# Attention outputs of two position blocks in one run of 128 products, with other buffer counts, a shared tile and another order

## The chip, the cores and the metric

The kernel runs on one core of one Trainium2 chip. The metric is the device time of one execution in microseconds (us), taken as the median of several executions. The core has five engines: TensorE (PE, matrix products; its weight loads appear as PEld), VectorE (DVE), ScalarE (ACT), GpSimd (POOL) and SyncE (SP, here an issuer of DMAs). Products land in eight accumulation banks of 128 x 512 float32; DVE or ACT must read a bank before it can be filled again.

## What is computed

The block reads x (2048 tokens of 448 features), normalises it, and sends the result through two branches: sliding dilated attention with 16 heads of 28, in which a token sees itself and the seven tokens at distances 2, 4, ..., 14 before it, and a GELU feed-forward of width 1792. The second branch, through a SiLU, gates the first.

```python
def _A_ref(x, wqkv, wo):
    H = 16; Dh = D // H
    W, dil = 8, 2
    q, k, v = ...
    idx = pos[:, None] - (jnp.arange(W) * dil)[None, :]
    ...
    attn = _softmax(logits, axis=-1)
    o = jnp.einsum("bhsw,bhswd->bhsd", attn, vg)
    return o.transpose(0, 2, 1, 3).reshape(B, S, D) @ wo

def _B_ref(x, w1, b1, w2, b2):
    h = _gelu(x @ w1 + b1)
    return h @ w2 + b2

xn = _layernorm(x, axis=-1)
return x + _A_ref(xn, ...) * _silu(_B_ref(xn, ...))
```

## The kernel before

**Positions.** Even tokens come first, then the odd ones, so that the dilation of 2 becomes a window of eight neighbouring positions. There are 16 tiles of 128 positions and 4 chunks of 512 (chunk c holds tiles 4c to 4c+3). Attention walks over nine blocks (the table VIS), here called visits: each has four sub-blocks of 57 query positions (56 in visit 4), each of which needs 64 key positions. Visit 0 begins at position 0, visit 4 at 912, visit 5 at 1136, visit 8 at 1820.

**Products.** Most products run with the 128 x 128 array split into two row tiles of 64 rows, two banks side by side (`pair`): L581 q and k projections, L604 the v projection, L657 the first feed-forward product (its result goes through GELU on ACT at L661), L689 the second feed-forward product, L849 the output projection. The last two tiles use the whole array (L711, L857).

**A visit** has two parts:

- "S": `scores_of` makes 32 products of 57 columns (L756, row tiles of 64, 128 columns of weights) into four banks. The keys were spread before into a buffer `kd` (L641 on ACT or L643 on DVE). `weights_of` then takes the exponentials of each bank on ACT into a buffer E (L765), and DVE multiplies E by the window's mask (L771).
- "P": `values_of` makes 64 products P V (L785, array split into 64-row by 32-column tiles) from four E buffers and a values buffer v into two banks. `output_of` then works on each of the two banks on DVE: transpose (L794), reciprocal of the row sums (L798), transpose back (L803), and the multiplication that writes oT and frees the bank (L808).

The values go from the v projection through a scratch tensor in HBM (v_hbm) and are loaded back in the layout of a visit by two DMAs (L391, from SP or POOL). k and q are turned by transposing DMAs from SP into qkT.

**Order.** The kernel builds a list of tasks, each with an engine, a modelled cost, dependencies, buffers that it takes and gives, and a priority. `_Plan.run` schedules this list once, when the program is built: at each step it takes the task that can start first, or one that can start within 0.12 us of it and has a higher priority. The numbers in PRIO, LATER and NUDGE are those priorities (NUDGE by the task's number). The instructions are then emitted in the planned order, and every engine runs its own in that order, waiting on semaphores. Buffers come from pools; p_b is the eight banks. A pool marked fifo hands its buffers out in the order in which the tasks were listed. E has 8 buffers of 512 columns, v has 3. The pool p_f with one entry and a task on an engine called "CLK" keep 3.5 us between the end of one P task and the start of the next in the plan.

`VISITS` lists the parts of a group of visits: S0, S1, P0, S2, P1, S3, and so on. The feed-forward of chunks 0 and 1 (first product) comes first, then visits 0 to 5 as one group, the first product of chunk 2, visits 6 to 8, and that of chunk 3. Exponentials of a group wait for the GELUs before it and GELUs for the exponentials before them, since ACT has to load another table. In `attn`, each S part depends on the S part before it and on the P part of the visit two earlier; each P part depends on its four masked exponentials, its values and the P part before it.

xnT holds the normalised x, turned (features on partitions, positions along the columns); oT holds the attention output in the same layout. Both are tiles of 4 x 2048 columns of their own. xnT of chunk c is read by the projections of its tiles and by the first feed-forward product of that chunk; oT is read by L849 and L857.

Of the kernel before, what the change touches and what calls it, by code (L numbers as in the profile page):

```python
# [17 lines left out]
TILED = 30  # L18
BURST = 3.5
NUDGE = {  # L20
    84: 158, 140: -205, 166: -239, 224: 179, 265: -119, 391: -219, 425: 30, 447: -224, 491: 168, 498: 19,
    903: 27,
}
LAST = 352
SAME = 20
# [2 lines left out]
MASK_ON = ("DVE", 0.4)  # L28


def VISITS(bs):
    out = []
    for i, b in enumerate(bs):
        out.append(("S", b))
        if i:
            out.append(("P", bs[i - 1]))
    return out + [("P", bs[-1])]

class _Pool:
# [138 lines left out]
def kernel(  # L180
# [13 lines left out]
    P = 128  # L194
    S, D, H, DH, F = A_x.shape[1], 448, 16, 28, 1792
# [4 lines left out]
    KT = 4  # L200
# [6 lines left out]
    HALF = S // 2  # L207
# [24 lines left out]
    def sb(name, shape, dt=BF16):  # L232
        return const.tile(shape, dt, name=name)
# [9 lines left out]
    b1r = sb("b1r", [P, P])  # L243
    b1 = sb("b1", [P, NMT], F32)
    b2 = sb("b2", [P, D])
    xnT = sb("xnT", [P, KT, S])
    qkT = sb("qkT", [P, 2, G, PAD + S])
    v_tok = [sb(f"v_tok{t}", [P, 2, H // 2, 32]) for t in range(4)]
    v_hbm = dram.tile([BACK + S, H * 32], BF16, name="v_hbm")
    oT = sb("oT", [P, KT, S])  # L250
    ident = sb("ident", [P, P])
    eps_t = sb("eps_t", [P, 1], F32)
    half_t = sb("half_t", [P, 4], F32)
# [32 lines left out]


    PRIO = {
        "project": (111.5, -88, 18.5, -696,),
        "project2": (-23.5, 19.5, -594, -964,),  # L290
        "values": (-44, -423, -594, -735.5,),
        "attn": (359, 96.5, 62.5, 202.5, 5, 57.5, 182.5, 179.5, 223.5,),
        "ff1": (13.5, 120, 49, 24, 187, 87.5, 62.5, -96, 84.5, 398.5, 78, 73.5, 5.5, 35, 103.5,
            101.5, 228.5, 177.5, -12.5, 185, 115.5, 165, -11, 8.5, 65.5, 138, 132.5, 110.5,),
        "gelu": (136.5, 97, 104.5, 181,),
        "ff2": (147, -34.5, -129, 114.5, 103, 89, -829, 135, -9.5, 180.5, -80, 104, 9, 131, -305.5,
            -310.5,),
        "final": (-14, 2, 199.5, -16.5, -12, -2, 22.5, 203, -185.5, 65.5, -11.5, 162.5, 193.5, 134,
            130, 176,),
        "norm": (131, 11, 219.5, 294, 126, 78, 2.5, 146.5, 217, -20.5, 87, 237, 173.5, 157, 14.5,  # L300
            120.5,),
        "loads": (-74, -48, 129, 164.5, 47.5, 92.5, 83.5, 53.5,),
        "stats": (49, 32, 205.5, 205.5, -8, 159.5, 204.5, 62, 27, 91, -57, 69.5, 123.5, 176.5, 85,
            125,),
        "turn_x": (198, 4.5, 200, 12.5, 117, 30.5, -154, 79.5, 36.5, 99.5, 169.5, 65.5, 252.5, 141,
            91, 50.5,),
        "turn_qk": (9, 28.5, 28, 90.5, 18, 3, 179.5, -13.5, 189.5, 20.5, 214, 5.5, 109, 113.5, 54,
            138,),
        "move_v": (111.5, 21, 150.5, -65.5, -155.5, 32.5, 203, 59.5, 78.5,),
        "store_v": (122.5, 143.5, 17.5, 49.5, 111, 48.5, 78, -15, 175, 108.5, 186.5, 121, 197.5,  # L310
            108.5, 47.5, 176.5,),
        "spread": (169, 63, 206, 112.5, 78, 182.5, 161.5, 83.5, 132.5,),
        "copies": (187, 4, 219, 15.5, 90, 177, 88.5, 31, 29, 20.5, 182, 51, 204.5, 49.5, 24,),
    }
# [431 lines left out]
    def scores_of(b):  # L746
        q, n = VIS[b]
        own, ready = spread(b)

        def fn(banks):  # L750
            for s in range(4):
                for g in range(G):
                    for h in range(2):
                        r = slice(64 * h, 64 * h + 64)
                        c0 = (G * (s % 2) + g) * n
                        nc.tensor.matmul(banks[2 * h + s // 2][:, c0:c0 + n], buf(p_k, own)[r, g, s, :],  # L756
                                         qkT[r, 0, g, PAD + q + n * s:PAD + q + n * s + n], start=True, stop=True)
        return fn, [ready] + [t_qk[t] for t in range(q // P, (q + 4 * n - 1) // P + 1)], ((p_k, own, 0),)
# [16 lines left out]
    def values_of(b, exps):  # L775
        n = VIS[b][1]

        def fn(banks):
            for s in range(4):
                for g in range(G):  # L780
                    for h in range(2):
                        for a in range(2):
                            r = slice(NK * a, NK * a + NK)
                            c0, c1 = (4 * h + s) * n, (G * (s % 2) + g) * n
                            nc.tensor.matmul(banks[a][32 * g:32 * g + 32, c0:c0 + n], buf(*v_at[b])[r, s, 2 * g + h, :],  # L785
                                             buf(p_E, exps[2 * h + s // 2])[r, c1:c1 + n], start=True, stop=True)
        return fn, tuple((p_E, e, 0) for e in exps) + (v_at[b],)
# [25 lines left out]
            t_oT[t].append(o)  # L813

    last_visit = {"S": [], "P": []}
    state = {}
# [225 lines left out]
```

## Time and profile before

| what | value |
|---|---|
| three executions | 152.68, 152.21, 152.67 us (median 152.67) |
| profiled execution | 152.89 us, of which the span of instructions is 151.20 us |
| granted TensorE clock | 0.998 of full speed |
| L657, L689 products | 392 of each; 44.0 and 40.2 us busy |
| L581, L604, L849 products | 25.4, 13.7 and 12.9 us busy |
| one P V run (L785, 64 products), nine in all | 0.70 us from its first product's start to its last one's end |
| one run of scores (L756, 32 products), nine in all | 0.59 to 0.61 us in the same sense |
| exponential (L765), 128 x 456 | 558 ns, 36 in all |
| mask (L771), 128 x 456 | 390 ns, 36 in all |
| output of one P V bank on DVE (L794, L798, L803, L808) | 677, 251, 678 and 633 ns |
| y addition (L723), 128 x 448, which frees an L689 bank | 619 ns |

The page gives the busy time of each engine and the chain of work that ended last. Matmuls overlap in the array, so a group's busy time can be longer than the distance at which the groups follow each other; the timeline, which merges neighbouring instructions of a kind into one line with its start and its duration to the end of the last, shows that distance. Groups of instructions are named by line, engine and the tiles written and read; "[0.43 <-DVE oT L808]" behind a line is the idle time before it and what ended it.

### The profile page before, as it was taken

To read this page: it belongs to the slowest core of one execution; us is meant where nothing else is said; L and a number is where in the kernel's file an instruction comes from. 1 tells how busy PE (TensorE), PEld (TensorE's weight loads), DVE (VectorE), ACT (ScalarE), POOL (GpSimd) and SP (SyncE) were. 2 spreads that over 40 slices of the span, in tenths; PEclk is the share of its full clock that TensorE was granted. 3 is DMA by queue.
4 is the path that set the end of the run, shared out by engine and by line. 5 is a ranking of instruction groups with operands and counts; after the bars stand their busy time and mean duration, and the time that the engine had idled before them with its cause. 6 is when DMAs were issued, how large, how long until landed. Compare 5 with 4: busy or idle time off the path is not lost.

```text
span 151.2 us, 5214 instructions
## 1 busy us (share of the span) xinstructions
PE 145.9 (97%) x2169; PEld 75.9 (50%) x2169; DVE 114.2 (76%) x277; ACT 93.7 (62%) x167; POOL 20.1 (13%) x53
## 2 busy tenths in 40 slices
PE   7899999999999999999998999999999999999990
PEld 2544444544455555555545554445556445555460
DVE  3886850585738789999598998587998977995952
ACT  3455888429893595767744679788296497822020
POOL 7435440214440000021200000000000000000000
PEclk9999999999999999999999999999999999999999
DMA  4999968899998357169699983421120000001221
GB/s 138 335 295 345 164 137 144 261 239 297 186 166 153 74 74 139 49 125 228 134 200 192 195 190 101 112 72 41 34 65 4 2 0 4 4 0 61 62 96 31
DMA packets 37895, 19.47 MB, mean 129 GB/s; under 512 B 24888, under 2 KB 37119, under 8 KB 37871
## 3 DMA queue, kind: packets, MB, share of 16 engines
q1 hardware_dynamic: 37118, 17.58, 51.9%
q0 software_dynamic: 608, 1.44, 4.3%
q8 instruction: 17, 0.28, 0.8%
q10 hardware_dynamic: 144, 0.11, 0.3%
q14 instruction: 8, 0.06, 0.1%
HBM read 9.42 MB, written 3.94 MB: 88 GB/s over the span
## 4 chain that ended last, share of the span: by engine, by line
PE 85%; DMA 5%; DVE 4%; POOL 3%; issue 1%; ACT 0%; POOLq 0%
PE bank L657 28%; PE bank L689 25%; PE bank L581 10%; PE bank L849 6%; DMA qkT<-qk_tok 5%; PE bank L604 4%; PE bank L711 4%; PE bank L785 3%; PE bank L756 2%; POOL wo L340 1%; DVE dt L803 1%; PE bank L857 1%; DVE dt L794 1%; PE bank L499 1%; DVE kd L643 1%
## 5 line engine op out<-in xcount | busy, mean ns | idle before, releaser
L657 PE MATMUL bank<-xnT,w 64*128 64x512 bf16 x392 | 44.0, 376 | 0.0
L661 ACT ACTIVATE h<-bank,b 128x512 bf16<-128x512 f32 x56 | 34.1, 688 | 10.3 <-PE bank L657 10.0
L689 PE MATMUL bank<-w,h 64*128 64x448 bf16 x392 | 40.2, 349 | 0.0
L657 PEld LDWEIGHTS <-w 64*128 64x128 bf16 x392 | 18.8, 94 | 22.1
L689 PEld LDWEIGHTS <-h 64*128 64x128 bf16 x392 | 18.8, 94 | 16.3
L581 PE MATMUL bank<-w_in,xnT 64*128 64x448 bf16 (+1 forms) x212 | 25.4, 350 | 0.0
L765 ACT ACTIVATE E<-bank 128x456 bf16<-128x456 f32 (+1 forms) x36 | 16.8, 557 | 6.4 <-PE bank L756 6.4
L333 ACT CAST qk_tok<-bank 128x448 bf16<-128x448 f32 x27 | 13.2, 538 | 6.7 <-PE bank L581 6.6
L794 DVE STREAM_TRANSPOSE dt<-bank 128x480 f32<-128x480 f32 (+1 forms) x18 | 12.1, 673 | 4.5 <-PE bank L785 4.4
L581 PEld LDWEIGHTS <-xnT 64*128 64x128 bf16 (+1 forms) x212 | 10.5, 94 | 9.6 <-issue 0.7
L604 PE MATMUL bank<-w_in,xnT 64*128 64x448 bf16 (+1 forms) x106 | 13.7, 349 | 0.0
L849 PE MATMUL bank<-wo,oT 64*128 64x448 bf16 x112 | 12.9, 349 | 0.4 <-DVE oT L808 0.4
L803 DVE STREAM_TRANSPOSE dt<-rd 128x480 f32<-128x480 f32 (+1 forms) x18 | 12.1, 675 | 0.6
L445 DVE BATCH_NORM_STATS2 st<-x_sb 128x6 f32<-128x448 bf16 x16 | 9.6, 609 | 3.1 <-DMA x_sb<-in_A_x_dram 3.1
L808 DVE TENSOR_TENSOR oT<-bank,dt 128x456 bf16<-128x456 f32 (+1 forms) x18 | 11.4, 632 | 0.6
L771 DVE TENSOR_TENSOR E<-E,m_gen 128x456 bf16<-128x456 bf16 (+1 forms) x32 | 11.0, 390 | 0.0
L723 DVE TENSOR_TENSOR y<-bank,b 128x448 f32<-128x448 f32 x15 | 8.7, 619 | 2.4 <-PE bank L689 2.2
L333 ACT CAST v_tok<-bank 128x448 bf16<-128x448 f32 x12 | 6.0, 534 | 5.6 <-PE bank L604 3.6
L735 ACT ACTIVATE t<-y 128x448 f32<-128x448 f32 x12 | 6.7, 582 | 3.9 <-DVE y L723 3.9
L849 PEld LDWEIGHTS <-oT 64*128 64x128 bf16 x112 | 5.6, 94 | 5.6 <-issue 0.9
L480 DVE TENSOR_SCALAR xn<-x_sb,mv,rstd 128x448 bf16<-128x448 bf16 x16 | 6.4, 399 | 2.4 <-POOL rstd L468 2.3
L604 PEld LDWEIGHTS <-xnT 64*128 64x128 bf16 (+1 forms) x106 | 5.6, 94 | 4.7
(74 smaller groups left out, 134.7 us busy)
## 6 DMA issues: line engine op xcount, KB each, us to landing
v_hbm<-v_tok SPq DMA_DIRECT2D x14, 128.0 KB, 3.9
out_dram<-o SPq DMA_DIRECT2D x15, 112.0 KB, 2.4
v<-v_hbm SPq DMA_DIRECT2D x13, 128.0 KB, 3.5
w<-in_B_w_dram SPq DMA_DIRECT2D x2, 672.0 KB, 7.1
w_in<-in_A_wqkv_dram SPq DMA_DIRECT2D x3, 336.0 KB, 4.4
x_sb<-in_A_x_dram SPq DMA_DIRECT2D x4, 224.0 KB, 5.5
w<-in_B_w_dram SPq DMA_DIRECT2D x2, 448.0 KB, 6.4
w<-in_B_w_dram SPq DMA_DIRECT2D x2, 336.0 KB, 5.8
```

Of the source, the lines that this page charges most:

```text
L333: nc.scalar.copy(o, i)
L581: return nc.tensor.matmul(ps[:, :D], xnT[r, kt, cs], w, start=start, stop=stop)
L604: return nc.tensor.matmul(ps[:, :D], xnT[r, kt, k0:k0 + P], w, start=start, stop=stop)
L657: return nc.tensor.matmul(ps[:], w1[r, kt, ms], xnT[r, kt, cs], start=start, stop=stop)
L661: nc.scalar.activation(buf(p_h, own, i)[:], buf(p_b, own, i)[:], ACT.Gelu_apprx_tanh, bias=b1[:, mt:mt + 1])
L689: return nc.tensor.matmul(ps[:, :D], buf(*h_at[(c, mt)])[r, cs], w2[r, mt, :], start=start, stop=stop)
L765: nc.scalar.activation(buf(p_E, k)[:, :8 * n], buf(p_b, a, at + i)[:, :8 * n], ACT.Exp, scale=SCALE)
L771: nc.vector.tensor_tensor(out=E, in0=E, in1=m[:, :, :, :n].rearrange("p i g q -> p (i g) q"), op=ALU.mult)
L794: nc.vector.transpose(buf(p_dt, k)[:, :32 * m], buf(p_b, po, i)[:, :32 * m])
L803: nc.vector.transpose(buf(p_dt, d)[:, :32 * m].rearrange("p (b c) -> p b c", c=32), buf(p_rd, r)[:, :m].unsqueeze(2).to_broadcast((P, m, 32)))
L808: nc.vector.tensor_tensor(out=oT[:, a::2, q:q + 4 * n1], in0=buf(p_b, po, i)[:, :n].rearrange("p (l q) -> p l q", l=2), in1=buf(p_dt, d)[: ...
L849: return nc.tensor.matmul(ps[:, :D], oT[r, kt, t * P:(t + 1) * P], wo[r, kt, :], start=start, stop=stop)
```

## The change

- `VISITS` now groups visits by TOGETHER: (0, 1), (2, 3), (4, 5), (6, 7), (8). It lists the S parts of a group, then the P part of the group before: S0, S1, S2, S3, P01, S4, S5, P23, P45; S6, S7, S8, P67, P8.
- A P part of two visits is one task of 128 products into four banks, which waits for the masks and values of both visits; it gives back eight E buffers and two v buffers. The four outputs follow as before, each for a bank.
- An S part of visit b depends on the S part before it and on the P task of the latest visit up to b - 4 that has one listed already.
- E has 15 buffers of 456 columns, v has 4.
- xnT and oT become two views of one tile xT of 4 x 3072 columns: oT is columns 0 to 2047, xnT columns 1024 to 3071. So positions 1024 and up of oT lie on positions 0 to 1023 of xnT.
- The numbers in PRIO, LATER and NUDGE are others, which gives another order on every engine.

```diff
 NUDGE = {
-    84: 158, 140: -205, 166: -239, 224: 179, 265: -119, 391: -219, 425: 30, 447: -224, 491: 168, 498: 19,
-    903: 27,
+    51: -17, 100: 72, 158: 186, 160: 19, 169: -108, 170: 110, 184: -158, 227: -173, 230: -199, 398: -138,
+    428: -8, 461: 105, 892: 15,
 }
...
+TOGETHER = ((0, 1), (2, 3), (4, 5), (6, 7), (8,))
+
+
 def VISITS(bs):
-    out = []
-    for i, b in enumerate(bs):
-        out.append(("S", b))
-        if i:
-            out.append(("P", bs[i - 1]))
-    return out + [("P", bs[-1])]
-
+    out, left = [], []
+    for m in [m for m in TOGETHER if m[0] in bs]:
+        out += [("S", b) for b in m] + left
+        left = [("P", m)]
+    return out + left
...
-    xnT = sb("xnT", [P, KT, S])
+    xT = sb("xT", [P, KT, HALF + S])
+    xnT, oT = xT[:, :, HALF:], xT[:, :, :S]
...
-    oT = sb("oT", [P, KT, S])
...
-    p_E = ring("E", 8, [P, 512], fifo=True)
+    p_E = ring("E", 15, [P, 8 * NW], fifo=True)
...
-    p_v = ring("v", 3, [P, 4, H // 2, 32], fifo=True)
+    p_v = ring("v", 4, [P, 4, H // 2, 32], fifo=True)
...
-        "attn": (359, 96.5, 62.5, 202.5, 5, 57.5, 182.5, 179.5, 223.5,),
+        "attn": (95, 33.5, 174.5, 3, 187.5, 61, 136.5, 427, 178.5,),
...
-    LATER = {"swap": 159, "qk": -43.5, "v": 16, "gelu": 21.5, "exp": 188.5, "mask": -4724.5, "pv": 29.5, "recip": 183.5, "os": 346, "y": 166, "tanh": 151, "g": 147.5, "sg": -120.5, "o": 0}
+    LATER = {"swap": 231.5, "qk": 165, "v": 171.5, "gelu": 94, "exp": 96.5, "mask": -4417.5, "pv": 209.5, "recip": 201.5, "os": 234, "y": 195, "tanh": 106, "g": 185.5, "sg": 100.5, "o": 89.5}
...
     def attn(b, what):
 
-        prio = PRIO["attn"][b]
         if what == "S":
+            prio = PRIO["attn"][b]
             fn, deps, give = scores_of(b)
-            a = plan.add("PE", 0.48, lambda k: fn([buf(p_b, k, i) for i in range(4)]), deps + state["early"] + last_visit[what][-1:] + last_visit["P"][b - 2:b - 1],
+            a = plan.add("PE", 0.48, lambda k: fn([buf(p_b, k, i) for i in range(4)]), deps + state["early"] + last_visit[what][-1:] + [value_of[e] for e in range(b - 3) if e in value_of][-1:],
                          prio, take=(p_b,) * 4, give=give, tail=0.15, mode=64)
             last_visit[what].append(a)
             state[b] = weights_of(b, a, 0, prio, state["gate"])
             return state[b][0]
-        exps, masked = state[b]
-        fn, give = values_of(b, exps)
-        a = plan.add("PE", 0.52, lambda k: fn([buf(p_b, k, i) for i in range(2)]), masked + t_v[b] + last_visit[what][-1:],
-                     prio + LATER["pv"], take=(p_b, p_b, p_f), give=give, tail=0.15, mode=33)
+        prio = PRIO["attn"][b[-1]]
+        parts = [values_of(e, state[e][0]) for e in b]
+        n = len(b)
+
+        def fn(k):
+            for i, (f, _) in enumerate(parts):
+                f([buf(p_b, k, 2 * i), buf(p_b, k, 2 * i + 1)])
+        a = plan.add("PE", 0.52 * n, fn, [d for e in b for d in state[e][1] + t_v[e]] + last_visit[what][-1:],
+                     prio + LATER["pv"], take=(p_b,) * (2 * n) + (p_f,), give=tuple(g for _, gs in parts for g in gs), tail=0.15, mode=33)
         plan.add("CLK", 0.0, None, [a], 300, give=((p_f, a, 0),), tail=BURST)
         last_visit[what].append(a)
-        for w in range(2):
-            output_of(b, a, w, w, prio)
+        for i, e in enumerate(b):
+            value_of[e] = a
+            for w in range(2):
+                output_of(e, a, 2 * i + w, w, prio)
         return []
```

The other lists of PRIO change in the same way as "attn".

More of the change, by code (lines that the diff above doesn't have):

```diff
@@ L288 @@
     PRIO = {
-        "project": (111.5, -88, 18.5, -696,),
-        "project2": (-23.5, 19.5, -594, -964,),
-        "values": (-44, -423, -594, -735.5,),
-        "attn": (359, 96.5, 62.5, 202.5, 5, 57.5, 182.5, 179.5, 223.5,),
[L293 to L312, printed above, removed]
+        "project": (136, 119.5, 53, -443.5,),
+        "project2": (38, -0, -278, -679.5,),
+        "values": (-43, -278, -332, -863,),
@@ new lines @@
+        "attn": (95, 33.5, 174.5, 3, 187.5, 61, 136.5, 427, 178.5,),
+        "ff1": (110.5, 186, 49, 159, -18.5, 129.5, 87, 189.5, 92, 142, 185, 18, 156, 198, 89, 31.5,
+            202.5, 86, 62.5, -70.5, 140, 20.5, 76.5, 126.5, -3, 181, 92, 212.5,),
+        "gelu": (120.5, -49.5, 86, -3,),
+        "ff2": (195, -34.5, -231.5, 114.5, 68.5, 89, 111.5, 135, 195, 180.5, 162, 104, 430, 131,
+            99.5, 28.5,),
+        "final": (128.5, 2, 1, -16.5, 41.5, -2, 41, 203, 110, 65.5, 194.5, 162.5, 189.5, 134, 208,
+            148,),
@@ new lines @@
+        "norm": (131, 11, 219.5, 294, 32, 66.5, 83.5, 207.5, 87.5, 115, 14, 127, 142.5, 64, 52.5,
+            80,),
+        "loads": (125, 117.5, -97.5, 131, 140.5, 12.5, 4, 84,),
+        "stats": (49, 32, 205.5, 205.5, 131.5, 117, 41, 114, 130, 91, 157, 32.5, 140.5, 101.5,
+            153.5, 258.5,),
+        "turn_x": (198, 4.5, 200, 12.5, 258.5, 205.5, 24.5, 200, 24.5, -25.5, 154, 60, 132, 183.5,
+            146.5, 78.5,),
+        "turn_qk": (187, 122.5, 29, 78, -20.5, -22.5, 153.5, -151, 65.5, 6.5, 138, 32, 198.5, 162,
+            35, 226.5,),
@@ L313 @@
+        "move_v": (146, 183, -68, 180, 92.5, 154.5, 241.5, 140.5, 190,),
+        "store_v": (175, 54, 86, -1.5, 139.5, 189.5, -0, 18.5, 82.5, 213, 109.5, -126, 116, 13,
+            53.5, 32,),
+        "spread": (92, 81.5, 89, 141, 58, 25.5, 142, 46.5, 42,),
         "copies": (187, 4, 219, 15.5, 90, 177, 88.5, 31, 29, 20.5, 182, 51, 204.5, 49.5, 24,),
     }
-    LATER = {"swap": 159, "qk": -43.5, "v": 16, "gelu": 21.5, "exp": 188.5, "mask": -4724.5, "pv": 29.5, "recip": 183.5, "os": 346, "y": 166, "tanh": 151, "g": 147.5, "sg": -120.5, "o": 0}
+    LATER = {"swap": 231.5, "qk": 165, "v": 171.5, "gelu": 94, "exp": 96.5, "mask": -4417.5, "pv": 209.5, "recip": 201.5, "os": 234, "y": 195, "tanh": 106, "g": 185.5, "sg": 100.5, "o": 89.5}
@@ L815 @@
     last_visit = {"S": [], "P": []}
-    state = {}
+    state, value_of = {}, {}
     def attn(b, what):
-        prio = PRIO["attn"][b]
         if what == "S":
+            prio = PRIO["attn"][b]
             fn, deps, give = scores_of(b)
-            a = plan.add("PE", 0.48, lambda k: fn([buf(p_b, k, i) for i in range(4)]), deps + state["early"] + last_visit[what][-1:] + last_visit["P"][b - 2:b - 1],
+            a = plan.add("PE", 0.48, lambda k: fn([buf(p_b, k, i) for i in range(4)]), deps + state["early"] + last_visit[what][-1:] + [value_of[e] for e in range(b - 3) if e in value_of][-1:],
                          prio, take=(p_b,) * 4, give=give, tail=0.15, mode=64)
```

## The prediction

> **What bounds the kernel now.** I read the page first: engine shares, slices, chain.
>
> ```profile
> span 151.2 us, 5214 instructions
> PE 145.9 (97%) x2169; PEld 75.9 (50%) x2169; DVE 114.2 (76%) x277; ACT 93.7 (62%) x167; POOL 20.1 (13%) x53
> PEclk9999999999999999999999999999999999999999
> PE 85%; DMA 5%; DVE 4%; POOL 3%; issue 1%; ACT 0%; POOLq 0%
> ```
>
> PE is busy 97% of the span at an undisturbed clock, and 85% of the chain that ended last is PE. A busy share can hide stalls, because ends of products are modelled, so I next read PE's instructions in order of time, and took the distances between the starts of neighbouring groups as their true cost.
>
> ```profile
> 51.75 0.92 PE L581 MATMUL bank<-w_in,xnT 64*128 64x448 bf16 x8
> 52.60 0.70 PE L785 MATMUL bank<-E,v 64*32 64x57 bf16 x64
> 53.23 0.74 PE L581 MATMUL bank<-w_in,xnT 64*128 64x448 bf16 x6
> ...
> 72.24 0.92 PE L581 MATMUL bank<-w_in,xnT 64*128 64x448 bf16 x8
> 73.00 0.73 PE L604 MATMUL bank<-w_in,xnT 64*128 64x448 bf16 x6
> 73.66 0.70 PE L785 MATMUL bank<-E,v 64*32 64x57 bf16 x64
> 74.29 1.50 PE L581 MATMUL bank<-w_in,xnT 64*128 64x448 bf16 x14
> ...
> 79.03 0.35 PE L849 MATMUL bank<-wo,oT 64*128 64x448 bf16 x1
> 79.81 0.91 PE L849 MATMUL bank<-wo,oT 64*128 64x448 bf16 x7 [0.43 <-DVE oT L808]
> ```
>
> Eight products of 64x448 that are followed by more of the same tile shape take 73.00 - 72.24 = 0.76 us. The eight ahead of a P V run take 52.60 - 51.75 = 0.85. So going into the run costs 0.09 us. The run holds PE for 53.23 - 52.60 = 0.63 us. Its last product ends at 52.60 + 0.70 and is 0.187 long (the L785 group's median), so it starts at 53.11: the 64 products start within 0.51 us, 8.0 ns apart, and the next product follows 0.12 later, 0.11 more than one such step. All nine runs are alike in this. A run therefore costs 0.09 + 0.51 + 0.12 = 0.72 us, of which 0.20 is change of tile shape. The only stall between 11 and 147 us is the last pair of lines: a product of the output projection starts 0.78 after its neighbour where a pair of products normally steps 0.19 on, so 0.59 us go to waiting for an attention output. In the waits this stall stands at 0.4, and behind the P V runs stand eight idle stretches of the weight loader, which has nothing to wait for but the change of shape:
>
> ```profile
> PEld L785 <- issue: 3.1, 8, 0.4
> ...
> PE bank L849 <- DVE oT L808: 0.4, 1, 0.4
> ...
> PEld L785 <- DMA v<-v_hbm: 0.4, 1, 0.4
> ```
>
> Last I read DVE, which has to give back the banks that P V fills: one output in order of time, and the busy times by stretch (the length first, then PE, PEld, DVE, ACT and POOL busy with their counts, then granted clock, DMA share, GB/s).
>
> ```profile
> 83.66 0.67 DVE L794 STREAM_TRANSPOSE dt<-bank 128x480 f32<-128x480 f32 x1
> 84.36 0.25 DVE L798 RECIPROCAL rd<-dt 128x15 f32<-128x15 f32 x1
> 84.65 0.68 DVE L803 STREAM_TRANSPOSE dt<-rd 128x480 f32<-128x480 f32 x1
> 85.36 0.63 DVE L808 TENSOR_TENSOR oT<-bank,dt 128x456 bf16<-128x456 f32 x1
> ...
> 60.00:85.00 25.00, 24.57 (x484) 13.53 (x482) 22.11 (x48) 15.30 (x33) 2.53 (x4) 1.00 0.70 162
> 85.00:105.00 20.00, 20.00 (x348) 10.06 (x340) 16.33 (x36) 16.91 (x29) 0.00 (x0) 1.00 0.48 101
> 105.00:120.00 15.00, 15.00 (x296) 8.61 (x294) 13.91 (x30) 9.71 (x18) 0.00 (x0) 1.00 0.13 36
> ```
>
> An output occupies DVE 2.25 us (83.66 to the next output's 85.91) and holds its bank that long. DVE is 22.11 of 25 us busy between 60 and 85, 13.91 of 15 between 105 and 120. PE sets the time, with DVE close behind in exactly the stretches where P V is done.
>
> **The change, part by part.** *Nine P V runs become five* (visits 0+1, 2+3, 4+5, 6+7, 8). The 576 products stay; four changes into the 64x32 shape and four out of it go. A merged run's second 64 products should cost 64 x 8.0 ns = 0.51, where a run of its own costs 0.72: 0.09 + (0.12 - 0.01) = 0.20 saved each by this reading. No run of 128 is in the trace. Bounds: if the second half cost a whole 0.63 again, only the way in is saved, 0.09 each, 0.36 in all; if it ran at about twice the pace of the whole run, 4 ns a product (0.26), 0.46 each, 1.84 in all. I take 0.20 each, the measured pace of the run itself, the nearest row there is; four give **0.80 us**.
>
> The Trainium skill (TensorE: Matmul & The Clock Gate, "Measured speedup vs the span model") states about 4 ns per further tile, by which a run of 64 would span 187 + 63 x 4 = 439 ns and four merges would bring the 1.84. Here the run spans 0.70 us from first start to last end, so the trace disagrees and its own pace stands in the sum.
>
> *P V takes four banks at once instead of two.* Four outputs of 2.25 us hold the last of them for 9.0 us of DVE alone, instead of 4.5. Until then PE has four banks: a pair of L657 or L689 products needs two, a visit's scores (L756) four. Nothing in a run itself gets longer; the price is waiting, bounded below by 0 (PE has products with two banks ready: 2.65 us of L689 per 28) and above by one stall like that of 79.2 us per merged run, 4 x 0.59 = 2.36 us. I take 0, as eight of the nine runs of the trace show no stall behind them.
>
> *The first visit of a pair waits for the second's masks.* Visit 0's P V, at 52.60 now, must wait for visit 1's scores (48.67), exponentials (four of 0.56, until about 51) and masks (0.39 each). On PE, in order, everything queued behind the run waits with it, and the final products (L849) that need its output come later; the cover is the other work of that stretch, at 0.095 us a product (28 of L689 in 2.65): 192 products L581/L604 for tiles 8 to 15 (18 us) and 224 of L689 for tiles 0 to 7 (21 us). I take 0. Without cover, one visit's four masks cost 4 x 0.39 = 1.6 us once.
>
> *15 buffers for exponentials, 4 for values.* The waits of ACT at L765 are for the scores' products alone (6.4 us), never for a buffer, so more of them remove nothing by themselves. Four visits ahead want 16; with 15 the fourth exponential of visit 3 waits until the first run is through, and behind it in ACT's order wait the casts (L333) that free banks; one such exponential is 0.56. Values loads (18 issues on SP and POOL, the same as now) may go out one visit earlier; the one wait for them (0.4, part of the weight loader's usual 0.39 of shape change) cost PE nothing. I take 0 for both.
>
> *Attention output over the spent columns of xnT.* Output positions from 1024 on lie over tiles 0 to 7. Their last readers, the L657 products of chunk 1, end at 40.46; the first such output follows the P V at 97.65. 57 us lie between, so a wait put there is long met: 0. The link from a visit's scores back to an earlier P V gets looser for visits 2 and 3 and reaches further back for the others: 0.
>
> *New order.* All priorities move, so which products stand around each wait is not shown. Below nothing: the one stall, 0.59. Above: the 2.36 already counted. I take 0.
>
> Sum: -0.80, within those bounds. The profiled execution has span 151.20 and took 152.89, 1.69 around it. 151.20 - 0.80 = 150.40; with 1.69 it is 152.09. The median of the runs shown, 152.67, lies 0.22 below the profiled one: **151.9**.
>
> **Rivals.** (1) *The saving lands and the stall goes too.* For it: the 0.59 is a matter of where one output projection stands. Against: the outputs come later now. 151.9 - 0.6 = 151.3.
>
> (2) *Banks and DVE take over (slower).* Place: behind merged runs between 60 and 92 and after 105 us. PE gets back one bank in 2.25 us, four in 9.0, while DVE must also take the y additions (0.62) that free L689's banks. For it: DVE at 88 and 93% there, and the stall at 79.2 is already PE waiting for L808. Against: ff1 pairs need no DVE, and PE never waited for a bank so far. At four stalls of 0.59: 152.67 + 2.36 - 0.80 = 154.2. It decides from 0.20 us of waiting per merged run, where the saving is eaten. The Trainium skill (TensorEngine Tiling, "PSUM Bottleneck") states that tiling speeds the products but not the evacuation of PSUM; the trace agrees, 0.63 us of run against 4.5 of outputs.
>
> (3) *Given back, no difference.* One more wait as long as the present one takes most of it: 152.67 - 0.80 + 0.59 = 152.5. For it: a saving of 0.80 is hardly more than one stall. Against: the eight stall-free runs.
>
> (4) *It doesn't merge in effect*: a second half as dear as a run, saving 0.36 in all: 152.3. Against: the 8.0 ns pace holds to the run's end.
>
> **How the numbers follow.** A measurement of this kernel can tell about 0.3% (0.46 us) from no change: 152.21 to 153.13 is the same. Forecast 0.44, rival (1) 0.13, (2) 0.26, (3) 0.10, (4) 0.07. Faster: 0.44 + 0.13 = 0.57; same: (3) and (4), 0.17, slower: 0.26. Range: the forecast's own is 151.2 to 152.2 (0.59 of stall and the low bound of the merge). Downwards nothing but the stall and a cheaper second half can be gained, so 151.1; upwards it takes in most of rival (2), to 154.3, leaving out its larger stalls, about 0.1, and less than 0.05 below.
>
> **What would show it.** In the changed profile: five P V runs, four of 128 products with about 1.14 us between their start and the next group's (1.26 would show rival 4), weight loads of L785 idle four or five times instead of eight or nine; PE without gaps over 0.3 us between 11 and 146; the span near 150.4 with PE's busy time near 145.1. Idle of PE put down to L808, L794 or L723 behind the merged runs would show rival (2). The prediction is wrong if PE idles over 0.8 us more than now, or if the span shrinks although PE's work between groups does not.

## The result, and the profile after

| | kernel before | changed kernel |
|---|---|---|
| executions | 152.21 to 153.24 us, median 152.68 (4) | 154.06 to 154.93 us, median 154.44 (4) |
| profiled execution | 152.89, span 151.2 | 154.93, span 153.2 |
| start of PE's last product | 147.49 | 149.53 |

The ratio is 1.0114 (95% interval 1.0087 to 1.0141): the change made the kernel slower by 1.1%. The profiled execution is the longest of the four. In all that follows, an execution over 1.5% above the fastest of its kernel counts as slow: the ratios leave it out, the medians and ranges do not. In the changed file the lines have moved by one to seven: ff1 is L658, ff2 L690, q and k L582, v L605, scores L757, P V L786, the outputs L795 to L809, exponentials L766, output projection L856, and the hop between the two halves of a pair L538.

The page of the changed kernel: span, engine shares, clock and the chain's shares by engine.

```profile
span 153.2 us, 5216 instructions
...
PE 146.5 (96%) x2169; PEld 82.8 (54%) x2169; DVE 116.9 (76%) x285; ACT 91.5 (60%) x159; POOL 20.0 (13%) x53
...
PEclk9999999999999999999999999999999999999999
...
PE 93%; DMA 2%; DVE 2%; issue 1%; ACT 0%; POOLq 0%
```

PE has the same 2169 products at the same clock, so the 2.0 us went into the distances between them. The timeline of PE, at three of the four merged runs:

```profile
58.64 1.28 PE L786 MATMUL bank<-E,v 64*32 64x57 bf16 x128
59.86 2.25 PE L582 MATMUL bank<-w_in,xT 64*128 64x448 bf16 x22
62.32 0.74 PE L582 MATMUL bank<-w_in,xT 64*128 64x448 bf16 x6 [0.20 <-issue]
...
86.85 1.37 PE L786 MATMUL bank<-E,v 64*32 64x57 bf16 x128
88.16 0.74 PE L605 MATMUL bank<-w_in,xT 64*128 64x448 bf16 x6
88.73 1.26 PE L658 MATMUL bank<-xT,w 64*128 64x512 bf16 x8
91.00 6.50 PE L658 MATMUL bank<-xT,w 64*128 64x512 bf16 x56 [1.00 <-POOLq L538]
...
127.03 1.28 PE L786 MATMUL bank<-E,v 64*32 64x57 bf16 x128
128.24 5.07 PE L658 MATMUL bank<-xT,w 64*128 64x512 bf16 x42
```

A merged run holds PE for 59.86 - 58.64 = 1.22 us (1.31, 1.21 and 1.21 for the others). Two runs of their own took 2 x 0.63 and one more way in, 0.09: 1.35. A merge thus saves 0.14 here, 0.55 if all four did, 0.45 in this execution; merged runs of the kernels below take 1.19 to 1.38 us, so not every one saves. The second half costs 0.58 (9.1 ns per product), not 0.51. The Trainium skill's rule of about 4 ns per further tile (TensorE: Matmul & The Clock Gate, "Measured speedup vs the span model") is measured there for up to 16 tiles; carried on to this run it gives an estimate of 187 + 127 x 4 = 695 ns. The trace has 1.28 us.

The stall of 0.59 us at the output projection of 79 us is gone. In its place there are gaps behind the merged runs, which the merged timeline mostly hides (its 6.50 us of 56 products has one inside). The chain of waits shows them, start and length of each step:

```profile
88.90 1.11 PE bank L658 x8
90.01 0.02 issue
90.03 0.03 POOLq L538
90.06 0.94 issue
91.00 1.70 PE bank L658 x14
92.70 0.02 issue
92.72 0.03 POOLq L538
92.75 0.05 issue
92.79 4.71 PE bank L658 x42
```

The products of a pair come in two halves. Between them its two accumulations change row tiles, and PE waits until a no-op on POOL (L538), the hop, has told that the first half is done. At 92.70 PE has made the first half of an ff1 pair, and its next instruction is that same pair's second half: product to product takes 0.49 us, where the pace is 0.216. I call this an open hop; it costs 0.27. In the kernel before another pair's half always stood between the two, and no hop was open. Here it is open four times (91.0, 92.8, 105.0 and 129.4, each time within 5 us of a merged run's end). At 91.0 PE waited another 0.89 us, 0.94 of "issue" after the hop had been told: for nothing that the profile shows. The gap at 62.3, 0.36 over the pace, is of that kind as well.

The waits of PE and its weight loader put nothing down to the outputs (L795 to L809) or to the y additions (L724):

```profile
PEld L658 <- POOLq L538: 2.4, 4, 0.6
...
PEld L786 <- issue: 1.9, 5, 0.4
...
PE bank L658 <- POOLq L538: 1.0, 1, 1.0
...
PE bank L582 <- issue: 0.2, 1, 0.2
```

Five changes into the P V shape instead of eight or nine, as forecast. The four hops are new. Last, DVE behind the run of 86.85 (first and last step of each of its four outputs):

```profile
87.61 0.68 DVE L795 STREAM_TRANSPOSE dt<-bank 128x480 f32<-128x480 f32 x1 [0.28 <-PE bank L786]
...
89.33 0.63 DVE L809 TENSOR_TENSOR xT<-bank,dt 128x456 bf16<-128x456 f32 x1
...
91.58 0.63 DVE L809 TENSOR_TENSOR xT<-bank,dt 128x456 bf16<-128x456 f32 x1
...
93.84 0.63 DVE L809 TENSOR_TENSOR xT<-bank,dt 128x456 bf16<-128x456 f32 x1
...
96.09 0.63 DVE L809 TENSOR_TENSOR xT<-bank,dt 128x456 bf16<-128x456 f32 x1
```

The four banks come back at 89.96, 92.21, 94.47 and 96.72, 2.25 us apart: half of PE's banks are gone at 88.2, one of them for 8.6 us more.

### The profile page after: what moved, and what is told of

Same layout as the page of the kernel before. It is cut to its first block, busy times and chain, and to the rows that moved or that the text cites. A ratio compares the mean times of both kernels' runs of the same rounds, so it can differ in the third digit from the quotient of the medians.

```text
span 153.2 us, 5216 instructions
## 1 busy us (share of the span) xinstructions
PE 146.5 (96%) x2169; PEld 82.8 (54%) x2169; DVE 116.9 (76%) x285; ACT 91.5 (60%) x159; POOL 20.0 (13%) x53
## 4 chain that ended last, share of the span: by engine, by line
PE 93%; DMA 2%; DVE 2%; issue 1%; ACT 0%; POOLq 0%
PE bank L658 28%; PE bank L690 24%; PE bank L582 14%; PE bank L605 7%; PE bank L856 7%; PE bank L786 4%; PE bank L712 4%; PE bank L757 3%; DMA x_sb<-in_A_x_dram 2%; PE bank L864 1%; DVE st L446 1%; PE bank L500 1%; DVE xn L481 0%; DVE xT L336 0%; DVE sg L876 0%
## 5 line engine op out<-in xcount | busy, mean ns | idle before, releaser
L658 PE MATMUL bank<-xT,w 64*128 64x512 bf16 x392 | 44.9, 376 | 1.3 <-POOLq L538 1.0
L690 PE MATMUL bank<-w,h 64*128 64x448 bf16 x392 | 39.8, 349 | 0.0
L658 PEld LDWEIGHTS <-w 64*128 64x128 bf16 x392 | 21.7, 94 | 22.0 <-POOLq L538 2.4
L690 PEld LDWEIGHTS <-h 64*128 64x128 bf16 x392 | 20.5, 94 | 15.7 <-issue 0.3
L582 PE MATMUL bank<-w_in,xT 64*128 64x448 bf16 (+1 forms) x212 | 24.7, 349 | 0.2 <-issue 0.2
L766 ACT ACTIVATE E<-bank 128x456 bf16<-128x456 f32 (+1 forms) x36 | 17.0, 557 | 4.8 <-PE bank L757 3.6
L334 ACT CAST qk_tok<-bank 128x448 bf16<-128x448 f32 x21 | 10.8, 535 | 12.8 <-PE bank L582 9.9
L582 PEld LDWEIGHTS <-xT 64*128 64x128 bf16 (+1 forms) x212 | 11.1, 94 | 9.4 <-POOLq L538 0.6
L795 DVE STREAM_TRANSPOSE dt<-bank 128x480 f32<-128x480 f32 (+1 forms) x18 | 12.1, 671 | 3.0 <-PE bank L786 2.9
L605 PE MATMUL bank<-w_in,xT 64*128 64x448 bf16 (+1 forms) x106 | 13.8, 350 | 0.1
L336 DVE CAST qk_tok<-bank 128x448 bf16<-128x448 f32 x11 | 6.7, 624 | 8.9 <-PE bank L582 8.8
L856 PE MATMUL bank<-wo,xT 64*128 64x448 bf16 x112 | 12.3, 349 | 0.0
L809 DVE TENSOR_TENSOR xT<-bank,dt 128x456 bf16<-128x456 f32 (+1 forms) x18 | 11.4, 632 | 0.6
L724 DVE TENSOR_TENSOR y<-bank,b 128x448 f32<-128x448 f32 x15 | 8.7, 618 | 4.1 <-PE bank L690 4.1
L856 PEld LDWEIGHTS <-xT 64*128 64x128 bf16 x112 | 6.6, 94 | 4.0 <-issue 0.4
L605 PEld LDWEIGHTS <-xT 64*128 64x128 bf16 (+1 forms) x106 | 5.9, 94 | 4.3 <-DVE xT L336 0.3
```

The costliest lines, as they stand in the source:

```text
L582: return nc.tensor.matmul(ps[:, :D], xnT[r, kt, cs], w, start=start, stop=stop)
L605: return nc.tensor.matmul(ps[:, :D], xnT[r, kt, k0:k0 + P], w, start=start, stop=stop)
L658: return nc.tensor.matmul(ps[:], w1[r, kt, ms], xnT[r, kt, cs], start=start, stop=stop)
L690: return nc.tensor.matmul(ps[:, :D], buf(*h_at[(c, mt)])[r, cs], w2[r, mt, :], start=start, stop=stop)
L766: nc.scalar.activation(buf(p_E, k)[:, :8 * n], buf(p_b, a, at + i)[:, :8 * n], ACT.Exp, scale=SCALE)
L795: nc.vector.transpose(buf(p_dt, k)[:, :32 * m], buf(p_b, po, i)[:, :32 * m])
```

## The experiments

Three theories. **INSTRUCTIONS**: a merged run is 128 weight loads and 128 products, 256 instructions in 1.2 us, and PE's supply of instructions runs dry behind it. **BANKS**: the four banks that a merged run holds leave no two free banks for a second pair, so the order planned behind it has to leave hops open. **ORDER**: the new order is only an unlucky one.

**1. Shifting the program against PE's instruction queue.** Counting PE's loads, products and semaphore instructions, the two gaps without a cause (62.3 and 91.0) fall behind instructions 1472 and 2496, which are 1024 apart; in both, PE goes on 1.45 us after the end of a 16 KB packet of its instruction queue (17 packets for some 4350 instructions, so 256 in each). So some ff1 products of chunks 0 and 1, long before the first run, were made in two halves of 256 columns each, which adds instructions but no columns: 56 products (112 instructions) in the changed kernel and the one before, 10 (20 instructions) in the changed kernel alone.

```diff
+                if x.n == CH and 0 < kt < 3 and n + m < size - 1 and left[0] > 0:
+                    cuts = [(slice(0, CH // 2),), (slice(CH // 2, CH),)]
+                    left[0] -= 2
```

> 56 of the first feed-forward products of chunks 0 and 1 are made in two halves of 256 columns, which puts 112 more PE instructions (a weight load and a product each) ahead of the first P V run and changes nothing behind it. Theory 'instructions': in the changed kernel's trace PE's instructions arrive in 17 packets of 16 KB, one per 256 instructions; a run of 128 products is 256 instructions and passes in 1.2 us, so PE comes to the end of what it has before the next packet lands. The two stalls of 0.36 us at 62.3 and 1.16 us at 91.0 stand 44 and 29 instructions behind a merged run, at the same place in the count of 256. Shifted by 112 the border falls into the middle of the runs, and the slow products on either side give the fetch its time: both stalls vanish, the split costs 0.1 to 0.3, so 153.0 to 153.3 against 154.4. Rival 'order' (banks, hops or DVE make these stalls): they stay, 154.4 to 154.8.

Measured: 154.3 us (153.96 to 154.55, six executions), ratio to before 1.010 (1.007 to 1.013). The profiled execution (154.5) no longer has the gaps of 62.3 and 91.0; it has the four open hops (90.6, 92.4, 104.5, 129.0) and one gap of 0.33 at 27.6, which is a wait for the normed x: the transposing DMA lands at 27.58, and PE goes on 0.04 later.

> The same with 10 products, 20 instructions. Theory 'instructions': the border comes nearer to the end of each run, to 24 instructions behind the first, 9 behind the second and some 30 behind the third, so the stalls grow to about 1.0 to 1.3, 1.7 to 2.2 and 0.6 to 1.2 us where they were 0.36, 1.16 and 0: 156.0 to 157.5. Rival 'order': nothing moves, 154.3 to 154.6.

Measured: 155.28 (154.12 to 156.75, four executions), ratio 1.014 (1.008 to 1.020): between the times that the two theories expected, and with one gap where INSTRUCTIONS expected three. Its profile is of the shortest execution; the gap of 62.3 is gone, the other one stands here, a group of products earlier in the program but again behind instruction 2496:

```profile
86.85 1.28 PE L801 MATMUL bank<-E,v 64*32 64x57 bf16 x128
88.07 0.55 PE L620 MATMUL bank<-w_in,xT 64*128 64x448 bf16 x4
88.85 0.36 PE L620 MATMUL bank<-w_in,xT 64*128 64x448 bf16 x2 [0.23 <-issue]
```

> The kernel before with the same 56 split products: what the splitting itself costs. It has no run of more than 64 short products (128 instructions in 0.63 us), so both theories expect no stall to come or go: 152.7 to 153.1.

Measured: 152.64 (152.35 to 153.49, ten executions), ratio 1.0003 (0.9978 to 1.0027): the halves cost nothing by themselves.

It follows that these gaps hang on the number of the instruction and not on the work that stands there, as INSTRUCTIONS has it. But with both gone the median fell by 0.1 only, and the kernel is still 1.0% slower than before, so they are not the main thing that makes it slower. How long they are in the executions without a profile isn't known; in the profile of after_split56, PE's last start fell by 0.43 only, since other waits (the one at 27.6, and 0.19 at 89.4) came in their place. The four open hops were in all three profiles of the changed order.

**2. Another order, and banks freed early.** Four kernels, whose orders were sought in the same way: additions to the priorities of 850 to 875 single tasks (NUDGE; half of them above some 140, the largest about 1000), chosen so that the planned end is early. In "merge_order2" it is the changed kernel's code, from the priorities of the kernel before. In "after_copy" and "before_copy" every P V bank is first copied to SBUF in bf16, which frees the bank, and the output steps read the copy; the buffers between those steps become bf16 as well:

```diff
-    p_dt = ring("dt", 2, [P, 512], F32)
-    p_rd = ring("rd", 2, [P, H], F32)
+    p_dt = ring("dt", 2, [P, 512])
+    p_ob = ring("ob", 2, [P, 480])
+    p_rd = ring("rd", 2, [P, H])
...
+        def f4(k):
+            copy(k.on, buf(p_ob, k)[:, :32 * m], buf(p_b, po, i)[:, :32 * m])
+        c = plan.add(("ACT", "DVE"), (act(32 * m), dve(32 * m)), f4, [po], prio + LATER["recip"] + 40, take=(p_ob,), give=((p_b, po, i),))
...
-            nc.vector.transpose(buf(p_dt, k)[:, :32 * m], buf(p_b, po, i)[:, :32 * m])
+            nc.vector.transpose(buf(p_dt, k)[:, :32 * m], buf(p_ob, c)[:, :32 * m])
...
-                                    in0=buf(p_b, po, i)[:, :n].rearrange("p (l q) -> p l q", l=2),
+                                    in0=buf(p_ob, c)[:, :n].rearrange("p (l q) -> p l q", l=2),
```

"before_t" is the kernel before with nothing but such additions.

> The changed kernel's code (merged runs, buffers, output over normed x) with another order: the priorities of the kernel before, and small additions to single priorities chosen so that the planned end is early. Three theories. BANKS: the four banks that a merged run takes come back one by one, some 2.25 us apart, as VectorE gets through their outputs, so no second pair of accumulators can be begun beside the first, and the hop between the two halves of a pair (0.27 us each) and the switch of engines stand open behind each merged run in whatever order: about four gaps of 0.45 to 0.5 us at L658, and 153.2 to 154.3 us. ORDER: the changed kernel's order was only an unlucky one; then another order has no such gaps, the merge shows its 0.55 us and the time is 151.9 to 152.7. INSTRUCTIONS: PE starves behind runs of 256 instructions: 154 or more, with gaps of 0.3 to 1.2 us behind merged runs where no semaphore is late.

Measured: 156.87 (154.06 to 159.41, four executions), ratio 1.015 (1.008 to 1.023) from the two of 154.06 and 156.12. The profile, of the shortest one, shows four open hops again (64.4 in a q and k projection, 90.4 in an output projection, 104.7 and 128.7 in ff1), a wait of the output projection for an attention output at 91.6 (0.26 over the pace), and no gap without a cause. That is what BANKS expected of the gaps, and against ORDER, as far as one more order can tell; the median lies above what BANKS expected. Even 154.06 is above the kernel before.

> Merged runs as in the changed kernel, but each P V bank is first copied to SBUF in bf16 (some 0.55 us on ScalarE, or VectorE), so that the bank is free at once, and the four steps of the output read the copy; its own order. BANKS: at most one open hop behind a merged run instead of four; last PE product near 147.5 and time 151.7 to 152.9, and no more than 0.3 above the same copies without the merge. INSTRUCTIONS: the gaps behind the merged runs (0.3 to 1.2 us, nothing late) remain, and the time is 1 us or more above the unmerged copies, and scatters by 1 us from run to run. Were the copies to load VectorE or ScalarE too much, both copies kernels would be slower alike.

Measured: 152.86 (152.47 to 153.33, ten executions), ratio to before 1.0009 (0.9994 to 1.0023). PE behind its second run:

```profile
86.09 1.28 PE L867 MATMUL bank<-E,v 64*32 64x57 bf16 x128
87.31 1.78 PE L686 MATMUL bank<-w_in,xT 64*128 64x448 bf16 x14
88.93 1.03 PE L739 MATMUL bank<-xT,w 64*128 64x512 bf16 x8
90.51 7.73 PE L739 MATMUL bank<-xT,w 64*128 64x512 bf16 x70 [0.55 <-DVE rd L885]
```

One open hop is left (88.35, inside the second line). ff1 pairs alternate from 88.93 on, as in the kernel before. The gap at 90.51, 0.71 over the pace, is put down to a reciprocal that no product reads; that reciprocal was done 0.44 us before PE went on. The gap falls behind instruction 2496, 1.45 us after a packet's end, the same place in the count as in the changed kernel.

> The kernel before with the same copies of the P V banks and its own order, single P V runs. All theories: 152.2 to 153.3, no gap of PE over 0.3 us after 12 us beyond the one or two of the kernel before. It is what the merged copies kernel is to be held against.

Measured: 152.89 (152.63 to 153.98, ten executions), ratio 1.0025 (1.0004 to 1.0046). Its profile is of an execution of 153.55; it has no open hop, and one wait of 0.61 for the normed x at 30.97, ahead of every P V run. With the banks freed early, merged and single runs are equal: 152.86 and 152.89. Without copies and with orders sought in the same way, they are 154.06 at best (merge_order2) and 151.98 (before_t, below). So the loss comes with the holding of the banks, as far as one order of each kind can show. The copies of after_copy add 6.6 us to ACT (12 at 555 ns) and 3.9 to DVE (6 at 654), and the last step of an output takes 396 ns from bf16 in place of 633. They are not free: with single runs, the copies kernel is 0.91 us above before_t.

> The kernel before with small additions to single priorities, as the others got them: shows what such a search for an order is worth by itself. All theories: 152.2 to 152.9; below 152.0 would mean that the search itself explains a gain of the others.

Measured: 151.98 (151.82 to 153.86, ten executions), ratio 0.9967 (0.9941 to 0.9993). Its profile has no gap of PE over 0.32 us after 11 us; the old stall is gone, and PE's last product starts at 146.86. This is the fastest kernel of the case, and it has single runs. A time below 152.0 was to mean that the search for an order can itself explain a gain of the others: half a microsecond between kernels of different orders says nothing sure about the merge.

**3. The merged runs cut in halves, all else kept.** The second visit's 64 products are emitted behind the next group of PE.

```diff
             for i, (f, _) in enumerate(parts):
-                f([buf(p_b, k, 2 * i), buf(p_b, k, 2 * i + 1)])
+                g = lambda f=f, i=i: f([buf(p_b, k, 2 * i), buf(p_b, k, 2 * i + 1)])
+                NEW.append(g) if i else g()
```

> The changed kernel with its order, banks and buffers, but the products of the second visit of each merged run are emitted behind the next group of products of PE (a first or second half of a pair), so that 128 products with their loads no longer come in one piece; the number of instructions is the same. Undoing the merge costs PE some 4 x 0.137 = 0.55 us, and one open hop (the one behind the run at 127) is covered by it, -0.27. INSTRUCTIONS (a run of 256 short instructions empties PE's supply): the gaps at 62.3 and 91.0 (0.36 and 1.16 us) go, the runs agree within 0.6 us, and the time is 153.0 to 153.9 in spite of the 0.55. If the gaps have another cause, they stay and the time is 154.4 to 155.2.

Measured: 154.84 (154.66 to 155.19, four executions), ratio 1.015 (1.014 to 1.017). The two gaps without a cause are gone, and three open hops are left, but the time did not fall: a miss. Part of the reason is a new wait. PE, then ACT, of its profile:

```profile
88.20 0.73 PE L793 MATMUL bank<-E,v 64*32 64x57 bf16 x64
88.86 0.39 PE L665 MATMUL bank<-xT,w 64*128 64x512 bf16 x1
89.70 2.60 PE L665 MATMUL bank<-xT,w 64*128 64x512 bf16 x19 [0.45 <-ACT E L773]
```

```profile
86.23 0.97 ACT L341 CAST v_tok<-bank 128x448 bf16<-128x448 f32 x2
89.10 0.55 ACT L773 ACTIVATE E<-bank 128x456 bf16<-128x456 f32 x1 [1.91 <-issue]
```

ACT stands 1.91 us before the last exponential of visit 5, which starts at 89.10, right after the second half of the run of visits 2 and 3 has ended (88.20 + 0.73). Visits 2 to 4 and the first three exponentials of visit 5 hold all 15 E buffers; the last one needs a buffer that this run gives back, and PE then waits for the bank that this exponential empties. In the changed kernel the same exponential starts at 88.37, behind the run's end (86.85 + 1.37), after 1.20 us of idle; there PE did not wait for it.

> The same edit on the merged kernel with the other order (154.06 to 159.41 in four runs, its profiled run, the shortest, with the four open hops and no other gap of PE). INSTRUCTIONS: the scatter is starvation behind the merged runs; in halves the runs lie within 0.8 us of each other, at 153.6 to 154.4 (its shortest run 154.06, +0.55 for the merges undone, -0.27 for the hop behind the run at 102). If the scatter has another cause (the order, a transfer), it stays: runs from 154 to 158.

Measured: 157.08 (156.12 to 157.99, four executions), ratio 1.030 (1.024 to 1.036); a miss as well. Its profile, of an execution of 157.84, shows a wait of another sort:

```profile
64.90 0.36 PE L667 MATMUL bank<-w_in,xT 64*128 64x448 bf16 x1 [1.68 <-DMA xT<-xn]
65.95 2.52 PE L667 MATMUL bank<-w_in,xT 64*128 64x448 bf16 x21 [0.69 <-ACT v_tok L419]
```

The v projection waits for the turned normed x of its tile: in this execution the transposing DMAs arrived too late for this order.

> The merged kernel with the other order once more, beside its version in halves on one chip. INSTRUCTIONS: scatter of 2 us or more again, median over 155, and a profile of a longer run shows gaps of 0.3 us or more behind merged runs with nothing to wait for, each some 1.2 to 1.5 us after a packet of PE's instructions ended. If the scatter belonged to the chip it ran on: within 1 us here, near 154.

Measured: 155.15 (153.64 to 158.09, four executions), on another chip than the first time; the three that enter the ratio (1.017, 1.012 to 1.022) are 153.64, 154.52 and 155.79. So the scatter is not that of one chip. Its profile is again of the shortest execution, with the four open hops alone, so what the long ones wait for was not seen in this kernel; late DMAs, as in its halved version, or instructions are both possible.

**4. Open hops by themselves.** The kernel before, with two blocks of two ff1 pairs put as first a, second a, first b, second b, where it had first a, first b, second a, second b.

```diff
+OPEN = ((732, 735), (857, 860))
...
+        order = list(self.order)
+        for first, second in OPEN:
+            t = next(t for t in order if t.seq == second)
+            order.remove(t)
+            order.insert(1 + next(i for i, u in enumerate(order) if u.seq == first), t)
```

> The kernel before, its runs single, with two of its blocks of two ff1 pairs (near 94 and 121 us) in another order on PE: first half a, second half a, first half b, second half b in place of first a, first b, second a, second b. So four hops stand open, as many as in the changed kernel; banks, buffers and all else as they were. If an open hop costs what its gap shows, the gaps of 0.49 us appear at four places of L657 (0.27 us over the usual 0.216 each) and the time is 153.6 to 153.9 (152.66 and 4 x 0.27). If PE makes up for them later, or if the gaps of the changed kernel come from the merged runs and not from the pairs standing alone, the time stays at 152.4 to 152.9.

Measured: 153.76 (153.61 to 154.55, seven executions) beside 152.81, ratio 1.0067 (1.0042 to 1.0093). In its chain of waits the first two look as in the changed kernel:

```profile
92.81 1.53 PE bank L663 x14
94.34 0.02 issue
94.36 0.03 POOLq L543
94.39 0.05 issue
94.44 1.70 PE bank L663 x14
96.14 0.02 issue
96.16 0.03 POOLq L543
```

All four gaps are 0.49. Four open hops cost 0.95 us (0.64 to 1.42) with single runs and nothing else changed. The gaps amount to 1.09, of which the old stall gave 0.39 back in this profile (0.59 over the pace became 0.20); the 0.70 that remain lie within that interval.

**5. Banks freed and the instructions shifted.** after_copy with the 56 split products of the first experiment.

> The merged kernel with copied banks, with 56 of its ff1 products of chunks 0 and 1 made in two halves of 256 columns (112 more instructions of PE ahead of the first merged run, which cost the kernel before nothing). In its profile PE stood at 90.5 us for some 0.7 us with nothing late, at its instruction 2497, 1.45 us after a packet of its instruction queue had ended. INSTRUCTIONS (the stall hangs on the count of instructions, and so another place of the program meets it): that gap is gone, and with no more than one of 0.3 us in its place the time is 152.1 to 152.6, 0.3 to 0.7 below the unsplit kernel, so that the merge shows its saving. If the gap belongs to this place of the program, it stays, and the time is 152.7 to 153.0.

Measured: 152.51 (152.19 to 153.72, twelve executions), ratio to before 0.9988 (0.9968 to 1.0008). The page's first line, and PE behind the run:

```profile
span 150.9 us, 5333 instructions
```

```profile
86.22 1.28 PE L882 MATMUL bank<-E,v 64*32 64x57 bf16 x128
87.44 1.78 PE L701 MATMUL bank<-w_in,xT 64*128 64x448 bf16 x14
89.06 3.19 PE L754 MATMUL bank<-xT,w 64*128 64x512 bf16 x28
```

There are 28 ff1 products in one piece where after_copy stood still after eight. The one open hop (88.5) is all that is left over 0.32 us after 11 us, and PE's last product starts at 147.04. Against the unmerged copies the ratios stand at 0.9988 to 1.0025, some 0.56 us. That is the size of the four merges (0.55), but the two intervals overlap a little, the orders differ, and an order alone can move the time as much (before_t): the saving fits and is not shown.

## Why the prediction was wrong

It forecast 151.9 us, and 151.1 to 154.3; measured were 154.44.

- **The merge: mechanism right, term mis-sized.** I took the pace of the run's first starts for the second half, 0.51; it costs 0.58. The saving is 0.14 a merge, 0.55 in all, not 0.80. (By its own terms the forecast's own range is 151.3 to 152.3, not 151.2 to 152.2; that changes nothing here.)
- **"P V takes four banks at once ... I take 0" is the step that failed**, together with **"New order ... I take 0"**. The reason given, that eight of the nine runs show no stall, held for runs of two banks. It also looked for the price in the wrong form: as PE idle behind L808 or L723. The order is fixed when the program is built, and it is built around a bank that would be late, so PE never meets it; the price appears as pairs that stand alone with their hop open, 4 x 0.27 = 1.09 us. That the hops have this price is shown by the fourth experiment; that they come with the holding of the banks is supported by the second (four of them in another order of the same code, one when copies free the banks, and no loss against single runs with the same copies). Why the planner leaves them open can be read from `_Plan.run` of the changed kernel, which works with modelled costs and needs no chip. Where the hops of 91.0, 92.8 and 129.4 stand in the plan, PE is through with the first half while seven of the eight banks are held, four, three and four of them by P V outputs; another pair needs two, and the second comes 0.24, 0.28 and 0.27 us later. At 105.0 no other pair is ready: the last pair of its chunk stands alone because its second bank came 0.25 too late one step before. On the chip this was not tried by itself.
- **Rival (2)** had the place (banks, behind merged runs) and nearly the time (154.2), but neither its stalls of 0.59 nor its signs came: no wait of PE is put down to an output.
- **The stall at 79** went, as rival (1) had it: -0.59. It is a matter of the moment as much as of the order: with the order of the kernel before, it was 0.59 in one profile, 0.20 in before_hops and under 0.1 in before_split56.
- **Not thought of: the supply of instructions.** 0.36 and 0.89 us in the profiled execution; how much in the others is open.
- **15 buffers for exponentials**: the wait of ACT behind the run is there (1.20 us before the fourth exponential, forecast as something to be hidden), and in the changed kernel it was hidden; moved 0.7 later, in after_halves, it stopped PE.
- **First visit waiting for the second's masks, oT over xnT**: 0, as taken; no wait for either is seen.

The 2.04 us by which PE's last start came later in the profiled execution (149.53 against 147.49) add up so: merges -0.45, old stall -0.59, open hops +1.09, instructions +1.25, two more changes of array shape near the end (the last tiles' second product, one group of 14 before, is now cut in two by eight of the output projection) +0.19, a later start of the split products at 11 us +0.19; 0.36 remain in gaps under 0.2 us, two of them after 112 us (0.16 and 0.1). The median lies 0.49 below the profiled execution; how much of the instructions' share the median holds was not traced.

## What to carry to other kernels

Where a schedule is fixed at build time, a scarce buffer doesn't show as a wait for that buffer but as a worse order: compare what stands between dependent pieces of work, and not only the waits. And ask the plan itself: by its modelled costs it ends at 150.30 us for the kernel before and 152.76 for the changed one, 152.01 for merge_order2, 150.50 and 150.52 for after_copy and before_copy, and 150.16 for before_t. The loss of the merge, the tie of the two copies kernels and the lead of before_t all stood there before any of these kernels ran; the prediction worked from the trace alone. Before merging two users of PSUM banks, count bank-time (here, at 2.25 us an output, the four outputs of a merged run hold their banks for 2.25, 4.5, 6.75 and 9 us, 22.5 us in all, against 2 x 6.75 for two runs) and shorten the holding first. And look at what an order can give alone: changed priorities alone brought the kernel before 0.33%, 0.5 us, about as much as the merge could have at best (0.55 us).

## What the runs showed of the hardware

PE seems to run out of instructions at times. Behind some runs of 256 short instructions it stood 0.36 to 0.89 us longer than its pace with every semaphore met, and went on 1.39 to 1.45 us after the end of a 16 KB packet of its instruction queue. Three kernels show it behind instruction 2496 (changed kernel, after_split10, after_copy), and it left that place when 112 instructions were put ahead (after_split56, after_copy_split). The Trainium skill (Runtime: NRT & Kernel Launch, "Instruction fetch mechanics") says that crossing a 16 KiB boundary is mostly hidden, since instructions are issued more slowly than they are fetched; at 4.8 ns per instruction (1.22 us for 256) the traces disagree. Why it is that number, and what decides how long the stall is in a given execution, stays open.

An order may also carry its own scatter: of merge_order2, the executions that enter the ratios spread over 2.1 us on each of two chips (two and three of them), the kernel before over 0.9 in 25 beside the first of them. What makes them differ was not seen.
